# Key-feature exponentials queued behind the logits' exponentials, later LN2 norms, and PV in paced vacant slots, in a fused attention and GLU kernel

## The chip, the cores and the metric

The kernel runs on one core of one Trainium2 chip. The metric is the device time of one execution in microseconds (us). Every time quoted is a median of several executions. One profile is taken of each kernel. Its span is about 1.7 us shorter than the time of the same execution.

Engines are named as the profile names them: PE (TensorE, matmuls), PEld (its weight loads), DVE (VectorE), ACT (ScalarE), POOL (GpSimd) and SP (SyncE, which issues most transfers).

## The reference

One block, in bf16, on 2048 tokens of width 448 with 16 heads of 28 and a hidden width of 1792: a modulated layer norm, an attention that works in four segments of 512 tokens and carries a memory from one to the next, a second modulated layer norm (LN2), and a gated linear unit.

```python
h = layernorm(x) * (1 + ca) + sa
# attention, per segment s; M and z start at zero
logits = q_s @ k_s.T * scale + causal_mask
a_dot = softmax(logits) @ v_s
pq = phi(q_s)                            # phi(t) = t + 1 if t > 0 else exp(t)
a_mem = (pq @ M) / (pq @ z + 1e-6)
o_s = g * a_mem + (1 - g) * a_dot        # g = sigmoid(beta), per head
pk = phi(k_s)
M, z = M + pk.T @ v_s, z + sum(pk)
# after all segments
x = x + ga * (o @ wo)
h = layernorm(x) * (1 + cb) + sb
x = x + gb * ((sigmoid(h @ w_gate) * (h @ w_up)) @ w_down)
```

## The kernel before

The work is cut into units (segment s, group hc of four heads). Each unit's logits come in three groups g. Between these groups PE is fed with jobs from a queue, `fill`, by their estimated cost: projections of later segments, the gated unit of earlier ones. `later(ns, fn, tag)` puts off the emission of an instruction by so many ns of estimated PE time; `need(tag)` emits at once what is still put off. Delays of `later` are therefore not waits on the chip: they decide an instruction's place in its engine's order.

The features phi of keys and queries are an exponential on ACT, then a max-add (r) and a minimum (e) on DVE. Those of keys are then transposed by a DMA from SP into pk, from which the memory's update dM is computed. Both `phi` and the causal masks on POOL follow each unit's logits:

```python
def phi(src, wait, tag, then=None):
    e = work.tile([P, L], BF16, tag="e", bufs=5, name="e")
    nc.scalar.activation(e[:], src, AF.Exp)

    def fin():
        r = work.tile([P, L], BF16, tag="r", bufs=2, name="r")
        nc.vector.tensor_scalar(r[:], src, 0.0, 1.0, op0=ALU.max, op1=ALU.add)
        nc.vector.tensor_tensor(e[:], e[:], r[:], ALU.min)
        if then:
            then(e)
    later(wait, fin, tag)
    return e

def mem_k(s, hc):                        # one key feature
    ...
    phi(kT_of[s][:, hc, :], 3500 if s < 2 else 5000, ("pk", s),
        lambda e: nc.sync.dma_start_transpose(pk[:, hc, :, :], e[:]))

def mem_update(s):
    need(("pk", s))
    ...                                  # 16 matmuls: dM += pk.T @ v

def logits(s, hc, g):
    ...                                  # matmuls into lg
    nc.scalar.activation(pT[:, :, w0:w0 + wid], lg[:, :, 0:wid], AF.Exp, scale=scale)
    if g == 0 and s > 0:
        pq_of[u] = phi(qT[:, hc, :], 3600, ("pq", u))
    for kb in KB_GROUPS[g]:
        later(2600, lambda kb=kb: mask(pT, kb), ("mask", u))

def wo_fin(s, t):                        # LN2 of tile t
    ...
    ln.stats(t)
    ln.rstd(t, t + 1)                    # on POOL
    later(1500, lambda: ln.norm_t(t), ("ln2", s))   # on DVE, then a transpose from SP

def mem_jobs(s):
    return [(0, lambda: [later((2000 if s < 2 else 2500) * hc, lambda hc=hc: mem_k(s, hc), ("pk", s))
                         for hc in range(NHC)])] + [(16 * TR, lambda: mem_update(s))]

def prep_b1():                           # modulation for the second half
    ga = mod_rep(2, 1.0, "ga")
    wm[4] = load_wm((nc.sync,), 4)       # 392 KB each, from SP
    gb = mod_rep(5, 0.5, "gb")
    wm[3] = load_wm((nc.sync,), 3)
    ...
def prep_b2():                           # matmuls that read wm[3] and wm[4]
    mod_cols(((3, 2), (4, 3)))

# the queue of the early jobs; j0..j3 are projections of segments 0 to 3, m[s] = mem_jobs(s)
fill.extend(j1[8:] + [(1800, prep_b1)])
fill.extend(j2[:8] + m[0][1:])
fill.extend(j2[8:] + j3[:2] + [(2000, prep_b2)] + j3[2:])

# main loop, for each unit and each g
logits(s, hc, g)
...
if prev[0] >= 0 and (g == 1 or g == 0 and s > 1 and pace[0] + debt <= 0) and prev in todo:
    pv(*prev)                            # 40 matmuls: softmax(logits) @ v
```

The softmax here doesn't subtract the row's maximum and nothing guards it: scores larger than these inputs give would overflow.

## Time and profile before

| | kernel before |
|---|---|
| time, median of the first 3 runs | 259.19 us (258.83 to 259.82) |
| span of the profiled run | 257.9 us |
| PE busy | 242.2 us (94%) |
| DVE, ACT, POOL busy | 68%, 54%, 29% |
| mean granted clock of PE | 0.993 |

PE is the bound, so the views to read are PE's order in time with its idle times and what ended each, and the granted clock in the same stretches. In a row of the timeline, "[0.74 <-DMA pk<-e]" means that PE stood idle for 0.74 us just before it and that a transfer into pk ended this. The rows are shown in the prediction below.

### The profile page before, as it was taken

What the parts mean: (1) busy time and instruction counts of PE and PEld (TensorE: products, weight loads), DVE (VectorE), ACT (ScalarE), POOL (GpSimd) and SP (SyncE); (2) the same over time, 40 slices, a digit from 0 to 9 for tenths busy, and PEclk for the clock granted to TensorE, in tenths of its full rate; (3) what the DMA queues carried; (4) which work ended last, traced back from release to release, by engine and by line L of the source; (5) the groups of instructions that cost most, each with busy time, mean ns of one, the idle gap of its engine ahead of it and who ended that gap; (6) DMA issues with size and microseconds to landing.
All of it is one profiled execution on the core that took longest, in us unless ns stands there. A gap on an engine that the chain in (4) does not pass through costs nothing.

```text
span 257.9 us, 5314 instructions
## 1 busy us (share of the span) xinstructions
PE 242.2 (94%) x2056; PEld 114.9 (45%) x2083; DVE 175.5 (68%) x419; ACT 139.8 (54%) x173; POOL 75.2 (29%) x140
## 2 busy tenths in 40 slices
PE   7899996989996979999999999999999999999994
PEld 2434543446533344444544355454353455333453
DVE  6878899586786677988858756895664586544412
ACT  0368888759886696856359666543663200133300
POOL 4368045144345031352502140362020023000000
PEclk9999999999998999999999999999999999999999
DMA  5999996664032024111322400114210015100011
GB/s 145 290 257 269 340 246 120 84 160 84 3 62 45 20 42 64 20 23 20 58 69 53 81 19 4 23 25 96 56 22 3 0 20 119 36 0 0 3 36 36
DMA packets 41169, 19.66 MB, mean 76 GB/s; under 512 B 30009, under 2 KB 40249, under 8 KB 41145
## 3 DMA queue, kind: packets, MB, share of 16 engines
q1 hardware_dynamic: 38408, 17.61, 31.3%
q10 hardware_dynamic: 2736, 1.72, 2.3%
q8 instruction: 16, 0.26, 0.4%
q14 instruction: 9, 0.07, 0.1%
HBM read 10.67 MB, written 1.84 MB: 48 GB/s over the span
## 4 chain that ended last, share of the span: by engine, by line
PE 46%; DVE 10%; issue 2%; POOL 1%; DMA 1%; ACT 1%; SPq 0%; DVEq 0%; POOLq 0%
PE ups L551 12%; PE dps L566 11%; PE gps L534 10%; PE gps L539 4%; PE acc L443 3%; DVE fT L554 2%; PE lg L418 2%; DVE st L269 1%; PE pwo L502 1%; DVE x_sb L512 1%; DVE ot L568 1%; DMA hT<-xn 1%; PE ups L539 1%; PE dM L391 1%; POOL rs L274 1%
## 5 line engine op out<-in xcount | busy, mean ns | idle before, releaser
L421 ACT ACTIVATE pT<-lg 128x2048 bf16<-128x2048 f32 (+1 forms) x48 | 76.7, 1598 | 25.9 <-PE lg L418 21.4
L429 POOL TENSOR_SCALAR_AFFINE_SELECT pT<-pT 128x512 bf16<-128x512 bf16 x64 | 41.7, 667 | 71.1 <-ACT pT L421 71.1
L542 ACT ACTIVATE tt<-gps 128x512 f32<-128x512 f32 x56 | 30.5, 594 | 56.1 <-PE gps L539 56.1
L554 DVE SCALAR_TENSOR_TENSOR fT<-tt,ups 128x512 bf16<-128x512 f32 x56 | 37.1, 687 | 34.1 <-PE ups L551 32.7
L566 PE MATMUL dps<-wd_sb,fT 128*128 128x448 bf16 (+1 forms) x238 | 44.1, 342 | 0.5 <-DVE ot L568 0.5
L534 PE MATMUL gps<-hT,wg_sb 128*128 128x512 bf16 x155 | 41.0, 387 | 1.4 <-DVE hT L291 0.5
L551 PE MATMUL ups<-hT,wu_sb 128*128 128x512 bf16 x164 | 40.6, 381 | 0.4 <-issue 0.3
L566 PEld LDWEIGHTS <-fT 128*128 128x128 bf16 x238 | 22.8, 98 | 19.2 <-issue 0.6
L534 PEld LDWEIGHTS <-wg_sb 128*128 128x128 bf16 x168 | 15.9, 99 | 19.1 <-issue 1.5
L551 PEld LDWEIGHTS <-wu_sb 128*128 128x128 bf16 x168 | 14.1, 98 | 21.5 <-issue 7.7
L443 PE MATMUL acc<-vt,pT 128*128 128x29 bf16 x640 | 18.7, 175 | 3.2 <-POOL pT L429 2.1
L443 PEld LDWEIGHTS <-pT 128*128 128x128 bf16 x640 | 17.7, 96 | 6.4 <-POOL pT L429 2.7
L273 POOL TENSOR_SCALAR rs<-mv 128x1 f32<-128x1 f32 (+2 forms) x21 | 5.4, 257 | 50.8 <-DVE mv L270 50.8
L269 DVE BATCH_NORM_STATS2 st<-x_sb 128x6 f32<-128x448 bf16 x32 | 19.7, 616 | 0.5
L418 PE MATMUL lg<-qT,kT 28*128 28x512 bf16 (+3 forms) x256 | 17.3, 302 | 1.5 <-ACT pT L421 1.5
L539 PE MATMUL ups<-hT,wgu_sb 64*128 64x512 bf16 x56 | 17.8, 382 | 0.7 <-DVE fT L554 0.5
L568 DVE TENSOR_TENSOR ot<-dps,x_sb 128x448 bf16<-128x448 f32 (+1 forms) x17 | 10.1, 593 | 11.6 <-PE dps L566 11.6
L343 PE MATMUL pq<-hT,wq_sb 128*128 128x512 bf16 x58 | 16.3, 380 | 1.3 <-DVE ou L452 0.9
L539 PE MATMUL gps<-hT,wgu_sb 64*128 64x512 bf16 x56 | 17.1, 382 | 0.1
L277 DVE TENSOR_SCALAR xn<-x_sb,mv,rs 128x448 bf16<-128x448 bf16 x32 | 14.1, 460 | 3.6 <-POOL rs L274 3.6
L343 PE MATMUL pq<-hT,wk_sb 128*128 128x512 bf16 x61 | 16.3, 379 | 0.3
L370 DVE TENSOR_TENSOR e<-e,r 128x512 bf16<-128x512 bf16 x24 | 13.7, 573 | 2.4 <-ACT pT L421 0.5
(101 smaller groups left out, 259.8 us busy)
## 6 DMA issues: line engine op xcount, KB each, us to landing
wm<-in_w_mod_dram SPq DMA_DIRECT2D x4, 392.0 KB, 6.5
x_sb<-in_A_x_dram SPq DMA_DIRECT2D x3, 448.0 KB, 5.9
wd_sb<-in_B_w_down_dram SPq DMA_DIRECT2D x3, 448.0 KB, 9.5
wg_sb<-in_B_w_gate_dram SPq DMA_DIRECT2D x3, 448.0 KB, 9.7
wu_sb<-in_B_w_up_dram SPq DMA_DIRECT2D x3, 448.0 KB, 11.2
out_dram<-ot SPq DMA_DIRECT2D x8, 112.0 KB, 1.9
out_dram<-ot ACTq DMA_DIRECT2D x7, 112.0 KB, 1.7
wm<-in_w_mod_dram SPq DMA_DIRECT2D x2, 196.0 KB
```

The costliest lines, as they stand in the source:

```text
L269: nc.vector.bn_stats(st[:], self.srcs[i])
L343: nc.tensor.matmul(pq[:, 0:L], lhsT=head_cols(w_sb, k, hc), rhs=h[:, k, :], start=(k == 0), stop=(k == NK - 1))
L418: nc.tensor.matmul(lg[:, hs, wid:wid + nq], lhsT=kT[r, hc, kb * P:(kb + 1) * P], rhs=qT[r, hc, kb * P:L], start=True, stop=True, tile_posi ...
L421: nc.scalar.activation(pT[:, :, w0:w0 + wid], lg[:, :, 0:wid], AF.Exp, scale=scale)
L429: nc.gpsimd.affine_select(out=blk, in_=blk, compare_op=ALU.is_ge, fill=0.0, base=0, pattern=[[0, 4], [1, P]], channel_multiplier=-1)
L443: nc.tensor.matmul(accv[:, qb, hs, 0:ME], lhsT=pT[:, hs, c0:c0 + P], rhs=vt[:, kb, hc * 4 + hs, 0:ME], start=(kb == 0), stop=(kb == qb))
L534: nc.tensor.matmul(g[:, 0:L], lhsT=wg_sb[:, k, f], rhs=h[:, k, :], start=(k == 0), stop=False)
L539: nc.tensor.matmul(dst[:, 0:L], lhsT=wgu_sb[r:r + LW, f], rhs=h[r:r + LW, 3, :], start=first, stop=not first, tile_position=(r, 0))
L542: nc.scalar.activation(tt[:], g[:, 0:L], AF.Tanh, scale=0.5)
L551: nc.tensor.matmul(u[:, 0:L], lhsT=wu_sb[:, k, f], rhs=h[:, k, :], start=False, stop=(k == 2))
L554: nc.vector.scalar_tensor_tensor(ft[:], tt[:], 1.0, u[:, 0:L], op0=ALU.add, op1=ALU.mult)
L566: nc.tensor.matmul(dp[:, c], lhsT=fT_of[(s, fc)][:, t * P:(t + 1) * P], rhs=wd_sb[:, fc, c], start=(fc == 0), stop=(fc == NFC - 1))
```

## The change

The intent is threefold. Exponentials of key features no longer come at fixed intervals, but one behind each exponential of a unit's logits (g = 1 or 2, or 0 in segment 0), so that they don't gather in front of the next one. (The recorded texts call these exponentials short. Only that of g = 2 is: in segment 0 of the changed kernel those of g = 0, 1 and 2 take 1.88, 1.91 and 1.08 us.) LN2's norms are put off longer, so that they don't hold up DVE. And PV may take a vacant slot at g = 0 in segment 1 as well.

```diff
-        phi(kT_of[s][:, hc, :], 3500 if s < 2 else 5000, ("pk", s), lambda e: ...)
+        phi(kT_of[s][:, hc, :], 3500, ("pk", s), lambda e: ...)
+    kq = deque()
     def mem_update(s):
+        while kq:
+            kq.popleft()()
         need(("pk", s))
 ...
         if g == 0 and s > 0:
             pq_of[u] = phi(qT[:, hc, :], 3600, ("pq", u))
+        elif kq:
+            kq.popleft()()
 ...
-        later(1500, lambda: ln.norm_t(t), ("ln2", s))
+        later(1500 if s == NSEG - 1 else 2400, lambda: ln.norm_t(t), ("ln2", s))
 ...
     def mem_jobs(s):
-        return [(0, lambda: [later((2000 if s < 2 else 2500) * hc, lambda hc=hc: mem_k(s, hc), ("pk", s)) for hc in range(NHC)])] + [(16 * TR, lambda: mem_update(s))]
+        return [(0, lambda: kq.extend([lambda hc=hc: mem_k(s, hc) for hc in range(NHC)])),
+                (16 * TR, lambda: mem_update(s))]
 ...
-    fill.extend(j2[:8] + m[0][1:])
-    fill.extend(j2[8:] + j3[:2] + [(2000, prep_b2)] + j3[2:])
+    fill.extend(j2[:8])
+    fill.extend(j2[8:10] + m[0][1:] + j2[10:] + j3[:2] + [(2000, prep_b2)] + j3[2:])
 ...
-                if prev[0] >= 0 and (g == 1 or g == 0 and s > 1 and pace[0] + debt <= 0) and prev in todo:
+                if prev[0] >= 0 and (g == 1 or g == 0 and s > 0 and (hc > 1 or s > 1) and pace[0] + debt <= 0) and prev in todo:
 ...
-                    fill.extend(tail)
+                    fill.extend((m[s][0:1] if s < 3 else []) + tail)
 ... (the first job of m[1] and of m[2] is taken out of its old place)
```

More of the change, by code (lines that the diff above doesn't have):

```diff
@@ L379, in mem_k @@
         pk = pk_of[s]
-        phi(kT_of[s][:, hc, :], 3500 if s < 2 else 5000, ("pk", s), lambda e: nc.sync.dma_start_transpose(pk[:, hc, :, :], e[:]))
+        phi(kT_of[s][:, hc, :], 3500, ("pk", s), lambda e: nc.sync.dma_start_transpose(pk[:, hc, :, :], e[:]))
     rm_of = {}
+    kq = deque()
     def mem_update(s):
+        if kq:
+            print("forced kq", s, len(kq))
+        while kq:
+            kq.popleft()()
         need(("pk", s))
@@ L796 @@
                             gj = gj[:8] + m[2][1:] + gj[8:]
-                            dj = dj[:3] + m[2][0:1] + dj[3:]
                         fill.extend(dj[:3] + h2_jobs(s - 1) + dj[3:] + gj)
                     else:
-                        fill.extend(h2_jobs(s - 1) + m[1][0:1] + gj[:8] + m[1][1:] + gj[8:])
+                        fill.extend(h2_jobs(s - 1) + gj[:8] + m[1][1:] + gj[8:])
                     pace[0] = (cost(fill) - KEEP[s] * GU) / (12 if s < 3 else 9)
```

## The prediction

> **What bounds the kernel now.** I began with the page: its shares of busy time, then its slices for the clock.
>
> ```profile
> PE 242.2 (94%) x2056; PEld 114.9 (45%) x2083; DVE 175.5 (68%) x419; ACT 139.8 (54%) x173; POOL 75.2 (29%) x140
> PE 46%; DVE 10%; issue 2%; POOL 1%; DMA 1%; ACT 1%; SPq 0%; DVEq 0%; POOLq 0%
> ```
>
> TensorE (PE) is busy for 94% of 257.9 us, and in the chain that ended last it has by far the largest share. So the kernel is bound by the order and density of PE's work, and a change that touches no matmul can win only the time in which PE stands still. Next I read PE's timeline for those places. Rows with an idle time and a releaser, in order of time:
>
> ```profile
> 40.02 1.15 PE L443 MATMUL acc<-vt,pT 128*128 128x29 bf16 x40 [1.11 <-DVE kT L348]
> ...
> 44.56 1.04 PE L343 MATMUL pq<-hT,wq_sb 128*128 128x512 bf16 x3 [0.89 <-DVE ou L452]
> ...
> 55.21 0.38 PE L391 MATMUL dM<-vt,pk 128*128 128x116 bf16 x4 [0.74 <-DMA pk<-e]
> ...
> 79.53 1.15 PE L443 MATMUL acc<-vt,pT 128*128 128x29 bf16 x40 [1.76 <-POOL pT L429]
> ...
> 82.01 1.03 PE L534 MATMUL gps<-hT,wg_sb 128*128 128x512 bf16 x2 [0.51 <-DVE hT L291]
> ...
> 91.98 0.40 PE L418 MATMUL lg<-qT,kT 28*128 28x384 bf16 x8 [1.30 <-ACT pT L421]
> ...
> 98.83 0.37 PE L539 MATMUL ups<-hT,wgu_sb 64*128 64x512 bf16 x1 [0.28 <-DVE fT L554]
> 99.43 0.37 PE L539 MATMUL ups<-hT,wgu_sb 64*128 64x512 bf16 x1 [0.20 <-DVE fT L554]
> ```
>
> These eight waits are 6.8 us. The columns are start, duration, engine and line, operation, and in brackets PE's idle time and what ended it. All lie before 100 us; behind that no single wait of PE reaches 0.5 us (0.34 at 124, 0.48 at 253). Whatever the change does in segments 2 and 3 is therefore worth nearly nothing: the prize lies in segments 0 and 1. Last, the busy time by windows around the wait at 79:
>
> ```profile
> 80.00:82.00 2.00, 1.50 (x32) 0.82 (x28) 0.63 (x2) 0.98 (x3) 1.23 (x2) 0.82 0.45 91
> 82.00:84.00 2.00, 1.89 (x4) 0.72 (x6) 1.93 (x7) 0.60 (x2) 0.00 (x0) 0.50 0.05 12
> 84.00:86.00 2.00, 1.88 (x12) 0.53 (x12) 0.88 (x3) 0.89 (x2) 0.00 (x0) 0.83 0.00 0
> ```
>
> The columns are busy time (and count) of PE, weight load, DVE, ACT and POOL, then granted clock, DMA share and GB/s. The clock fell to half from about 81.3 to 84.7 us, just behind the idle stretch; that costs at most 3.4 x 0.5 = 1.7 us more.
>
> **What the Trainium skill says.** "TensorE: Matmul & The Clock Gate", Part 1: the clock is halved after an idle window of about 3.4 us, and the windows run freely. The trace agrees in the length (0.82, 0.50 and 0.83 over 6 us make 3.4 us at half); that a window with 1.76 us of waiting suffices is this trace's own finding. The same page, under "Architectural detail", calls ACT and DVE strict FIFO; the trace agrees, as an exponential of key features at 92.33 stands ahead of the one of the logits at 92.85, whose logits began at 91.98. "DMA: Bandwidth & Descriptors", section "Queues, rings and completion order": each DMA engine takes the descriptors of a ring in order. The trace fits: a transpose usually lands 2.4 us after its issue, but the one of oT issued at 55.16, behind the two 392 KB loads of wm (54.05 and 54.69), landed at 59.98, after 4.8 us.
>
> **The change part by part.** It adds no work: the order of the built programs has the same 4168 rows on PE, and on the others the same operations, moved. PE's order differs in two places only: dM of segment 0 comes after two tiles (8 matmuls) of the v projection instead of before them; and one PV (40 matmuls, of unit 2 of segment 1) comes before the second logits of unit 3 instead of after. The extended condition thus moves a single PV.
>
> 1. *Key features of segment 0, on DVE.* Each costs DVE one max-add and one min, by the rows of kT here 0.28 + 0.43 to 0.67 us. One pair (36.49 to 37.30, 0.8 us) stands before the kT copy of 39.31 that PE's PV waits for; in the new order it is behind it. The copy comes some 0.7 us earlier, limited by its own matmul: PE's wait of 1.11 shrinks to about 0.4, worth **0.7 us**. A second pair (41.80 to 42.85) stands between that PV and its ou (43.88); it moves behind it, so ou comes about 1 us sooner and the wait of 0.89 goes: **0.9 us**.
>
> 2. *dM of segment 0.* Its four pk tiles come by DMA transposes in the SP queue, one issue each 1.3 us (43.66, 45.05, 46.33, ...: the queue issues nearly back to back from 41 to 56 us). Now the exponentials stand one behind each short exponential, so the fourth is at about 45 us instead of 38.1, and its fin on DVE at about 49 instead of 45.1. In the new SP order the two wm loads and one oT come before the fourth pk, and the wm loads before the third. Before, the fourth pk was issued at 52.73 and landed at 55.17. If all else stays, it is issued after two loads (1.1 us) and one oT (1.3 us) more, less up to 1.5 us of gaps that close: about 53.6. It then lies behind 784 KB of loads; the oT of before took 4.8 us in that place, and those further back 4.0. So it lands at some 55.5 to 57.5, say 56.2. PE wants it: before at 54.4; two tiles later (+1.6), less the 1.6 of point 1, again at about 54.3. So a wait of roughly 1.9 to 2.3 takes the place of 0.74: **-1.3 us** as an estimate, and this is the least certain term.
>
> 3. *Later LN2 norms.* In segment 1 a norm with its copy (0.39 + 0.18 us) leaves the stretch of DVE before the last statistics (75.26). POOL's masks stand in its order behind the rs that waits for these statistics (idle 2.68 us at 76.19), and PE's PV at 79.53 waits for the masks. So PE gains about **0.55 us**. The last norm now follows the third in the time in which it waited for POOL (0.76 us), so hT isn't later; the wait at 82.01 stays. In segment 2 hT was ready at 132.05 and wanted at 134.14, which leaves room. In segment 3 it was ready at 180.33 and wanted at 180.68: 0.35 us of slack only, and I allow 0.1 of loss there.
>
> 4. *PV in the vacant slot, and the exponentials of segment 1.* At 90.69 PE had nothing but the second logits, which wait until ACT has emptied the first. ACT began that exponential at 90.05, behind one of key features (89.53), though its logits began at 88.68. Now the key feature isn't there: ACT can begin when its two tanh end (89.65), 0.4 us earlier. And the PV, 1.0 us of PE, whose masks were done at 87.8, fills the rest. 1.30 + 0.1 of pipeline refill: **1.4 us**.
>
> 5. *fT.* At 98 PE waits for buffers that DVE frees with fT at 98.10, behind two key-feature pairs (95 and 97). One pair moves behind the first fT pair and one leaves: the 0.48 us of the two waits go, with the gaps between starts perhaps 0.8. I take **0.6 us**.
>
> Sum: 0.7 + 0.9 - 1.3 + 0.55 - 0.1 + 1.4 + 0.6 = 2.75 us. As PE bounds everything after 100 us, this should pass to the end undiminished.
>
> **The rivals.** *(a) The new wait for pk is no worse than the old one*, because SP closes more gaps or the loads are done sooner. For it: 8 matmuls more were put ahead of dM for just this purpose. Against it: the order of SP and the late oT above. Then 1.3 to 2 us more are won: 254.4 to 255.2. *(b) The wait for pk is 3 us or more, and PE's clock falls there.* For it: 1.76 us sufficed at 79. It would cost up to 1.7 us: with 1 us of longer wait 258 to 259. *(c) The fall of the clock at 81 goes*, as the wait there shrinks from 1.8 to 1.2 us: up to 1.3 us won, since part of the half-speed window was idle anyway. The windows run freely, so this may differ from run to run, and the runs before spread by 1 us (258.83 to 259.82). *(d) ACT becomes the bound of 40 to 50 us*: it was busy for 14.6 of the 20 us from 40 to 60, and a fourth exponential now stands ahead of the q copy at 45.6. Some of point 1 would be lost, but as PE then waits for pk anyway, that costs nothing more.
>
> **Range and chances.** The median before is 259.19; less 2.75 is 256.4. (b) and (c) about balance, and (a) at one chance in four with 1.6 us pulls by 0.4; I allow half of that, as (d) pulls the other way: 256.2. All gains with (a) and (c) reach 253.3; only the PV with a bad wait and a slow clock gives 258.5. I put 8 in 10 at 253.9 to 258.4. Faster by over 2% needs under 254.0, so (a) together with most of (c): 0.11. Slower by over 2% (over 264.4) has no mechanism that I see: 0.02.
>
> **What would show it right or wrong.** Right: PE's waits at 40, 44.6, 92 and 98 gone or under 0.4 us; the PV of segment 1's third unit standing at 90 directly behind mem, followed by logits with no wait; the wait for masks near 77 at 1.2 to 1.3 us; a wait of dM for pk of about 2 us, with the third and fourth pk landing 3 us or more after their issue behind wm; no new PE wait over 0.4 us after 100 us. Wrong: if dM waits under 0.8 us, point 2 fails and the time is near 255; if it waits over 3, or a half-clock window stands at 55 us, the time is near 258. If hT of segment 3 arrives more than 0.5 us late, point 3 fails. And if these waits are gone but the span isn't shorter, PE wasn't the bound after 100 us.

## The result, and the profile after

The changed kernel is correct and took 262.75 us (median of 4 runs, 261.99 to 263.53) against 259.1 us for the kernel before. The ratio is 1.0136, with a 95% interval of 1.0095 to 1.0178. A ratio is the mean time of one kernel's runs over that of the other's runs of the same rounds, so not quite the ratio of the medians. The change made the kernel 1.4% slower. The prediction said 256.2 us, with 258.4 as the end of its range: it had the wrong sign.

The profile below is of the slowest of the four runs (263.53 us); the one of the kernel before is of a run of 259.59 us. The mean clocks of the four were 0.98, 0.992, 0.98 and 0.992. One window of 3.4 us at half clock takes 0.0065 off the mean of such a span; so, by this estimate, the profiled run's 0.98 means three such windows (two and one, below), and 0.992 about one, wherever it stood. The two runs of 0.992 took 261.99 and 262.25 us, still some 3 us more than the kernel before, whose profiled run had one window too. The term for the clock below is that of the profiled run, and larger than in these two.

From the page of the changed kernel, the busy times, the granted clock in 40 slices of 6.5 us, and the shares of the chain that ended last:

```profile
PE 245.6 (94%) x2056; PEld 115.9 (44%) x2083; DVE 175.7 (67%) x419; ACT 139.6 (53%) x173; POOL 75.6 (29%) x140
...
PEclk9999999985999799999999999999999999999999
...
PE 56%; DVE 8%; POOL 2%; issue 2%; ACT 1%; DMA 1%; DVEq 0%; POOLq 0%
```

PE has the same 2056 instructions but is busy for 3.4 us longer: some ran at half clock. The clock row shows where, at the slices of 52 to 65 us and of 85 to 91 us. PE is still the bound.

PE's timeline of the changed kernel, at the places shown before and at new ones (start, duration, engine, line, operation, and idle time before it with what ended it):

```profile
39.03 1.15 PE L451 MATMUL acc<-vt,pT 128*128 128x29 bf16 x40 [0.38 <-DVE kT L348]
...
42.92 1.02 PE L343 MATMUL pq<-hT,wq_sb 128*128 128x512 bf16 x3 [0.23 <-PE lg L424]
...
56.91 0.38 PE L397 MATMUL dM<-vt,pk 128*128 128x116 bf16 x4 [2.79 <-DMA pk<-e]
58.16 0.57 PE L397 MATMUL dM<-vt,pk 128*128 128x116 bf16 x4 [0.86 <-DMA pk<-e]
...
83.53 1.15 PE L451 MATMUL acc<-vt,pT 128*128 128x29 bf16 x40 [1.71 <-POOL pT L437]
...
94.34 1.16 PE L451 MATMUL acc<-vt,pT 128*128 128x29 bf16 x40
95.43 0.40 PE L424 MATMUL lg<-qT,kT 28*128 28x384 bf16 x8
...
143.41 0.39 PE L547 MATMUL ups<-hT,wgu_sb 64*128 64x512 bf16 x1 [0.49 <-DVE t L463]
...
186.73 0.39 PE L547 MATMUL ups<-hT,wgu_sb 64*128 64x512 bf16 x1 [0.52 <-DVE t L482]
```

The waits of 1.11, 0.89, 1.30, 0.28 and 0.20 are gone or small, as predicted. But dM's 0.74 became 2.79 + 0.86 = 3.65 us, the wait for masks did not shrink, and there are waits beyond 100 us that were not there before. The busy time by windows around dM (columns: busy time and count of PE, weight load, DVE, ACT, POOL, then granted clock, DMA share, GB/s):

```profile
54.00:56.00 2.00, 0.12 (x3) 0.00 (x0) 0.00 (x0) 0.26 (x1) 0.16 (x1) 1.00 1.32 271
56.00:58.00 2.00, 0.38 (x4) 0.22 (x4) 0.00 (x0) 0.00 (x0) 0.00 (x0) 0.88 0.98 188
58.00:60.00 2.00, 1.84 (x11) 0.79 (x12) 1.24 (x3) 0.61 (x1) 0.51 (x1) 0.50 0.08 16
60.00:62.00 2.00, 2.00 (x7) 0.81 (x6) 1.88 (x2) 2.00 (x3) 1.52 (x2) 0.50 0.01 4
```

All engines stand almost still from 54 to 58 us while the DMA engines are full; then PE works at clock 0.50 until about 64.35 us, which is two windows of 3.4 us.

The quickest way to place a loss is to compare the start of the same logits in both timelines. The difference, after minus before (taken before rounding), can only change where PE gained or lost:

| logits of (segment, unit, group) | before, us | after, us | lag, us | step, us | what lies between |
|---|---|---|---|---|---|
| 0, 0, 0 | 16.92 | 16.66 | -0.26 | | |
| 0, 3, 0 | 46.39 | 44.73 | -1.66 | -1.40 | DVE order in segment 0 |
| 1, 0, 0 | 57.04 | 58.66 | +1.62 | +3.28 | dM's wait for pk |
| 1, 1, 0 | 65.31 | 69.61 | +4.31 | +2.69 | half clock at 57.5 to 64.4 |
| 1, 2, 0 | 74.46 | 78.50 | +4.05 | -0.26 | LN2 norms |
| 2, 0, 0 | 99.73 | 101.26 | +1.53 | -2.52 | PV slot, fT; clock at 85 about equal |
| 3, 0, 0 | 144.20 | 147.19 | +2.99 | +1.46 | segment 2 |
| 3, 3, 1 | 186.33 | 190.29 | +3.95 | +0.96 | segment 3, at its end |

From there the lag stays to the end, as it does in all kernels below.

### The profile page after: what moved, and what is told of

It reads as the page before. It is cut to its first block, busy times and chain, and to the rows that moved or that the text cites. A ratio compares the mean times of both kernels' runs of the same rounds, so it can differ in the third digit from the quotient of the medians.

```text
span 261.8 us, 5314 instructions
## 1 busy us (share of the span) xinstructions
PE 245.6 (94%) x2056; PEld 115.9 (44%) x2083; DVE 175.7 (67%) x419; ACT 139.6 (53%) x173; POOL 75.6 (29%) x140
## 3 DMA queue, kind: packets, MB, share of 16 engines
q10 hardware_dynamic: 2736, 1.72, 2.3%
HBM read 10.67 MB, written 1.84 MB: 48 GB/s over the span
## 4 chain that ended last, share of the span: by engine, by line
PE 56%; DVE 8%; POOL 2%; issue 2%; ACT 1%; DMA 1%; DVEq 0%; POOLq 0%
PE ups L559 14%; PE dps L574 13%; PE gps L542 12%; PE gps L547 5%; PE acc L451 3%; PE pwo L510 3%; PE lg L424 3%; DVE fT L562 1%; POOL pT L437 1%; ACT pT L427 1%; DVE ot L576 1%; DMA hT<-xn 1%; DVE x_sb L520 1%; PE ups L547 1%; DVE st L269 1%
## 5 line engine op out<-in xcount | busy, mean ns | idle before, releaser
L343 PE MATMUL pq<-hT,wq_sb 128*128 128x512 bf16 x58 | 17.0, 393 | 0.8 <-issue 0.4
L355 PE MATMUL pv<-wv_sb,hT 128*128 128x448 bf16 x64 | 15.4, 389 | 0.0
```

The costliest lines, as they stand in the source:

```text
L343: nc.tensor.matmul(pq[:, 0:L], lhsT=head_cols(w_sb, k, hc), rhs=h[:, k, :], start=(k == 0), stop=(k == NK - 1))
```

## The experiments

All kernels gave correct results. Most edits below are to the changed kernel.

**Were the wm loads to blame for dM's wait?** First the issues of transfers between 47 and 60 us (size in KB, median us from issue to landing), of the kernel before:

```profile
wm<-in_w_mod_dram SPq DMA_DIRECT2D x2, 392.0 KB, 4.1
...
pk<-e SPq DMA_TRANSPOSE x2, 2.4
```

and of the changed kernel, followed by SP's own timeline there:

```profile
wm<-in_w_mod_dram SPq DMA_DIRECT2D x2, 392.0 KB, 4.3
pk<-e SPq DMA_TRANSPOSE x3, 4.6
```

```profile
51.14 1.07 SPq L120 DMA_DIRECT2D wm<-in_w_mod_dram  x2
52.30 1.20 SPq L380 DMA_TRANSPOSE pk<-e  x1
53.55 1.27 SPq L498 DMA_TRANSPOSE oT<-ou  x1
54.91 1.22 SPq L380 DMA_TRANSPOSE pk<-e  x1
```

The third and fourth pk now stand behind both loads. The profile has landings for one pk in each of these stretches: 2.4 us for that of 52.73 before, 4.6 us for the third now. The fourth let PE go on at 58.16, 3.25 us after its issue. In e1 both loads are issued after the last pk, in e1b only one of them, and e2 leaves the wait but fills it with 16 matmuls whose result is thrown away, so that the clock can't fall.

```diff
 # e1                                       # e1b: the wm[3] line alone
-        wm[4] = load_wm((nc.sync,), 4)
-        wm[3] = load_wm((nc.sync,), 3)
 ...in mem_update
         need(("pk", s))
+        if s == 0:
+            for j in (4, 3):
+                wm[j] = load_wm((nc.sync,), j)
 # e2, in mem_update, ahead of the third pk
+            if s == 0 and hc == 2:
+                idle = m_f32("idle")
+                for _ in range(16):
+                    nc.tensor.matmul(idle[:, 0:L], lhsT=ident[:], rhs=hT_of[("1", 2)][:, 0, :], start=True, stop=True)
```

> The changed kernel, with its two 392 KB loads of wm issued on SP behind the fourth pk of segment 0 instead of ahead of the third; the exponentials stay where the change put them. Theory A (the transposes of pk queue behind the loads): the third and fourth pk land about 2.5 us after their issue, dM waits for pk under 1 us instead of 2.79 + 0.86, no half-clock windows stand at 57 to 64 us, and 262.75 falls by about 2.7 + 2.6 to 257 or 258. Theory B (the exponentials queued behind each short one come too late, the loads are innocent): dM still waits over 2 us, the clock still falls, and the time stays at 262 or more.

> The changed kernel with one of the two wm loads (the second) moved behind the pk transposes, the other left ahead of them: the dose between the changed kernel (both ahead, waits for pk 2.79 and 0.86 us) and e1 (none ahead, wait 2.02, no half-clock window). Theory (each load that stands ahead delays the transposes by its own share): wait about 2.8 us in sum, one half-clock window, 260 to 261 us, ratio 1.004 to 1.008. Rival (only the order in the queue counts, not the bytes: one issue of 0.6 us): wait 2.6 to 2.7 at most and no window, ratio 1.002 or less. Other rival (one load is as bad as two): as the changed kernel, 1.012.

> The changed kernel with 16 dummy matmuls of 512 columns (3.45 us, their result is not used) between the second and third head group of dM in segment 0, where PE waits for pk. Nothing waits less, so without a clock effect the time is that of the changed kernel, 262.7, or a little more. Theory A' (the empty stretch of PE makes the clock fall for the next two windows): the clock stays at full speed from 54 to 65 us and the time falls by about 2.6 us to 260.1. Rival (the clock falls for another reason): still two half-speed windows near 57 to 64 us, and 262.7 or more.

| kernel | time, us | ratio to before (95%) | dM's wait, us (profiled run) | half-clock windows behind it (profiled run) |
|---|---|---|---|---|
| changed | 262.75 | 1.0136 (1.0095 to 1.0178) | 3.65 | 2 |
| e1b, one load ahead | 261.64 | 1.009 (1.005 to 1.0129) | 1.84 + 0.78 = 2.62 | 2 |
| e1, none ahead | 258.69 | 0.999 (0.9951 to 1.0029) | 2.02 | 0 |
| e2, wait filled | 261.91 | 1.0112 (1.0077 to 1.0148) | 0.64 beside the fill | 0 |

dM in e1's timeline, and the windows there:

```profile
56.09 0.38 PE L400 MATMUL dM<-vt,pk 128*128 128x116 bf16 x4 [2.02 <-DMA pk<-e]
```

```profile
54.00:56.00 2.00, 0.07 (x2) 0.00 (x0) 0.00 (x0) 0.01 (x1) 0.00 (x0) 1.00 0.40 81
56.00:58.00 2.00, 1.91 (x15) 1.02 (x16) 1.49 (x3) 1.08 (x1) 0.76 (x1) 1.00 0.86 216
```

The loads cost 1.6 of the 3.65 us, and with them, in the profiled runs, come the two windows at half clock. The remaining 2.0 us is SP's queue: in e1 the last pk is still issued only at 53.6 us, because the pk, hT and oT transposes leave SP one per 1.3 us. Neither of the two theories given for e1 was right in all: A in the landings (2.4 us) and the clock, not in its wait of under 1 us; B in a wait of over 2 us, not in the clock. e1b shows that the clock falls with a wait split in two parts of 1.84 and 0.78 us as well; it was slower than its theory said (260 to 261). e2 shows the clock's part in its profiled run: with the same long stretch at dM, but filled, no window at half clock follows, and at the third logits of segment 1's first unit its lag is 1.44 us where the changed kernel has 4.31. At the start of segment 3's second unit it is -0.2 against +2.99; 0.3 us of this comes of the window at 85 us, which e2's run lacks too. Its time missed the theory (261.91 instead of 260.1): 1.4 us was lost again in segment 3, where its step is +2.34 us instead of +0.96 (a late transpose; last section), and four of its six runs had mean clocks of 0.985 to 0.992, so that they had windows somewhere.

How many windows follow is not fixed by the wait. e3 and e12 (below) have the program of the changed kernel up to this place. In their profiled runs dM waited 2.98 + 0.82 and 3.28 + 0.73 us, longer than in the changed kernel, and one window at half clock followed instead of two: 1.63 and 1.69 us of lag, where the two cost 2.69.

**Is segment 0 the whole difference?** e10 puts segment 0 alone back: key features of s = 0 at the old intervals, dM at its old place.

```diff
+        if s == 0:
+            return [(0, lambda: [later(2000 * hc, lambda hc=hc: mem_k(s, hc), ("pk", s)) for hc in range(NHC)]), (16 * TR, lambda: mem_update(s))]
-    fill.extend(j2[:8])
-    fill.extend(j2[8:10] + m[0][1:] + j2[10:] + j3[:2] + ...)
+    fill.extend(j2[:8] + m[0][1:])
+    fill.extend(j2[8:] + j3[:2] + ...)
```

> The changed kernel with segment 0 alone put back: its key features at the old fixed intervals, dM at its old place, the rest of the change kept. Theory (the loss is the sum of its places: segment 0 with dM's wait and the two half-clock windows +4.2, norms -0.3, PV slot and fT -2.3, segment 2 +1.5, segment 3 +1.0): minus 4.2 against the changed kernel, so 258.5 to 259.2, ratio about 1.000, with dM's wait about 0.7 us and no half-clock window at 57 us. Rival (segment 0's waits only push a later loss about, so that what is won there is given back): 261 or more.

It took 257.38 us, ratio 0.994 (0.9899 to 0.9981), with a wait of 0.19 us at dM and a mean clock of 1.0. So segment 0 turns the change from a gain into a loss. It did 1.1 us better than the theory's 258.5. In its trace the step in segment 2 was 0.3 us instead of 1.5, though the order there is that of the changed kernel; dM's wait was 0.19 us where 0.7 was expected; and there is no half-clock window near 81 us, as there is in the kernel before.

**What was lost in segment 2?** e4 puts the key features of segment 2 back to the old intervals.

> The changed kernel with the key features of segment 2 alone put back to the times of before (every 2500, fin after 5000, begun after three down jobs). Theory D (the waits of PE at 138.0 and 143.4 us, 0.36 and 0.49, come of the key-feature pairs of segment 2 standing ahead of the copies that free PSUM on DVE): those waits go and the time falls by 1.2 to 1.5 us, to about 261.3. Rival (they come of the later norms): unchanged, 262.7.

It took 261.9 us, ratio 1.0091 (1.0053 to 1.0129); theory D had said 261.3. In its trace the lag stays constant through segment 2 (0.36 to 0.30 us): the 1.5 us are due to the new order of segment 2. But e10 has that order and lost little. The same stretch in DVE's timeline of the changed kernel, then in POOL's:

```profile
140.80 0.76 DVE L369 TENSOR_SCALAR r<-qT 128x512 bf16<-128x512 bf16 x1
141.59 0.73 DVE L370 TENSOR_TENSOR e<-e,r 128x512 bf16<-128x512 bf16 x1
```

```profile
140.78 1.27 POOL L437 TENSOR_SCALAR_AFFINE_SELECT pT<-pT 128x512 bf16<-128x512 bf16 x2 [2.62 <-ACT pT L427]
```

and of e10, again DVE, then POOL:

```profile
134.90 0.28 DVE L369 TENSOR_SCALAR r<-qT 128x512 bf16<-128x512 bf16 x1
135.22 0.42 DVE L370 TENSOR_TENSOR e<-e,r 128x512 bf16<-128x512 bf16 x1
```

```profile
135.24 1.49 POOL L437 TENSOR_SCALAR_AFFINE_SELECT pT<-pT 128x512 bf16<-128x512 bf16 x2 [2.62 <-ACT pT L427]
```

In the changed kernel the pair of query features starts 20 ns after two masks on POOL and takes 1.49 instead of 0.70 us. In e10 it starts first, and the masks take 1.49 instead of 1.27. Only the masks have moved: the pair starts 0.88 and 0.87 us after PE's PV in the two traces, the masks 0.86 and 1.21 us after it. The Trainium skill states this in "SBUF — State Buffer", section "Who interferes with whom": a DVE instruction in a two-port mode contends with GpSimd, one with two inputs in SBUF with a GpSimd instruction that reads SBUF, and whichever issues first holds the other up. The trace agrees in both directions. Behind the slowed pair stand the three instructions that free the accumulator of PV, for which PE then waited 0.49 us. This was tested by moving that pair alone; on no other engine does the order change.

```diff
 # e12
-            pq_of[u] = phi(qT[:, hc, :], 3600, ("pq", u))
+            pq_of[u] = phi(qT[:, hc, :], 4600 if u == (2, 3) else 3600, ("pq", u))
```

> The changed kernel with one pair of DVE instructions (max-add and min of the query features of segment 2's fourth unit) moved behind the three that free the accumulator for PE; nothing else moves on any engine. Theory (segment 2's larger wait, 0.49 us at 143.4, comes from DVE and GpSimd meeting: the pair took 0.76 + 0.73 us beside two masks at 140.78 to 142.05, against 0.28 + 0.42 in the same order where they do not meet): the wait of 0.49 goes, the step of 0.77 us in the lag between the second and the third logits of that unit goes, and 0.7 to 0.8 us of it reaches the start of segment 3; the wait of 0.36 us at 138 stays. In the time -0.3%: ratio about 1.010. Rival (the accumulator's release is late for another reason, such as the late release of the two buffers before it): the step stays at 0.5 us or more.

In e12's DVE timeline the pair is back at its usual length:

```profile
140.94 0.28 DVE L369 TENSOR_SCALAR r<-qT 128x512 bf16<-128x512 bf16 x1
141.25 0.42 DVE L370 TENSOR_TENSOR e<-e,r 128x512 bf16<-128x512 bf16 x1
```

The wait of 0.49 us is gone, and the step between the second and the third logits of the unit is -0.10 instead of +0.77 us. The other, 0.7 us before the second logits, stayed, as expected. The time was 261.94 us, ratio 1.01 (1.0064 to 1.0136). e12 by itself doesn't tell the collision from the order, as it also takes the pair's ordinary 0.70 us out of the way. e10 does: there the pair stands in the changed kernel's place at its usual length, PE has no wait of 0.49 us, and the lag stays at -3.68 between the second and the third logits. The two together show that half of segment 2's loss (0.77 us) is the collision. The other half comes with the new order too (e4 removes it); 0.36 us of it is a wait behind DVE, in which a pause of 0.46 us between r and e stands that no run explains. e10 hasn't this pause, and its step there is 0.39 instead of 0.75 us.

**LN2's norms.** e11 is the kernel before with the later norms alone, e3 the changed kernel with the norms of segment 2 (whose LN2 runs during segment 3) at the old 1500.

```diff
 # e11, on the kernel before
-        later(1500, lambda: ln.norm_t(t), ("ln2", s))
+        later(1500 if s == NSEG - 1 else 2400, lambda: ln.norm_t(t), ("ln2", s))
 # e3, on the changed kernel
-        later(1500 if s == NSEG - 1 else 2400, lambda: ln.norm_t(t), ("ln2", s))
+        later(2400 if s < 2 else 1500, lambda: ln.norm_t(t), ("ln2", s))
```

> The kernel before with the later LN2 norms alone (2400 instead of 1500, the last segment left). The prediction's step: the wait for masks near 79 us shrinks by 0.55 us and that passes to the end, 258.4, ratio 0.998. Theory after seeing the two traces: only about 0.3 us, 258.7, ratio 0.999, which five rounds hardly tell from nothing; so the trace decides: the wait at 79.5 us 1.76 in the kernel before, 1.2 by the prediction, 1.5 by the later theory.

> The changed kernel with the LN2 norms of segment 3 (those of s = 2) deferred by 1500 again, as before the change; segments 1 and 2 keep 2400. Theory C (three hT transposes now queue behind each other at 175.7 to 178.3 us, and what comes of it is PE's wait of 0.37 at 184.9 and 0.52 at 186.7): both waits shrink under 0.3 us and the time falls by 0.7 to 1.0 us, to about 261.9. Rival (these waits come of DVE's order around the key features of segment 2 or of chance): no change, 262.7.

e11 took 259.55 us, ratio 1.0021 (0.9985 to 1.0058). Its PE rows:

```profile
79.01 1.18 PE L443 MATMUL acc<-vt,pT 128*128 128x29 bf16 x40 [1.70 <-POOL pT L429]
...
180.89 0.81 PE L534 MATMUL gps<-hT,wg_sb 128*128 128x512 bf16 x3 [0.37 <-DVE ot L568]
...
182.75 0.39 PE L539 MATMUL ups<-hT,wgu_sb 64*128 64x512 bf16 x1 [0.52 <-DVE t L474]
```

The wait for masks is as long as before (1.76), and the two waits of the changed kernel's segment 3 are there. So this part alone wins 0.26 us of order in segment 1 and loses 1 us in segment 3. The masks' wait stays because no norm left the place ahead of the last statistics: In the kernel before, DVE has a norm at 74.09 and these statistics at 75.26; in e11 it has one at 73.34 and the statistics at 74.51. Each norm only moved down by one place, and the one before it took its place. Why it loses is seen on SP and DVE. The changed kernel, SP, then DVE:

```profile
174.41 0.33 SPq L577 DMA_DIRECT2D out_dram<-ot  x1
175.74 3.81 SPq L287 DMA_TRANSPOSE hT<-xn  x3
```

```profile
180.90 0.74 DVE L291 TENSOR_SCALAR hT<-hT,cols 128x512 bf16<-128x512 bf16 x2 [3.72 <-DMA hT<-xn]
```

The later norms put the last three transposes behind an output and back to back, 1.3 us each. The last lands at 180.8 us, and DVE, whose next instruction needs it, waits 3.72 us (3.00 before) with everything behind it. e3 took 262.06 us, ratio 1.0124 (1.0079 to 1.0168): in its trace the waits and the step of 0.96 us are gone, as theory C said, but the time moved by less than the spread that the clock makes (its runs had mean clocks of 0.974 to 0.987).

**PV's slot.** e5 is the kernel before with the new condition for PV alone.

```diff
-  (g == 1 or g == 0 and s > 1 and pace[0] + debt <= 0)
+  (g == 1 or g == 0 and s > 0 and (hc > 1 or s > 1) and pace[0] + debt <= 0)
```

> The kernel before with one part of the change alone: the PV of segment 1's third unit in the slot ahead of the second logits of its fourth. Theory E (the slot was empty: PE waited 1.30 us there for ACT): that wait shrinks to about 0.5, as the exponential of key features still delays ACT, PE is about 1.0 us ahead at the third logits of that unit, and the time falls by 0.8 to 1.0 us to about 258.1. Rival (what is won is lost at once in the two waits for fT at 98 us, since DVE isn't faster): these waits grow from 0.48 to over 1 us and the time falls by less than 0.4 us.

It took 257.44 us, ratio 0.9952 (0.992 to 0.9984). Its lag against the kernel before goes from -0.50 us at the start of the third unit of segment 1 to -2.34 at the start of segment 2, and stays; 0.36 us of this comes before the slot, 1.49 in it and behind it. PE's wait of 1.30 us became 0.30 there and 0.47 at the next logits, and the two waits for fT are gone, though the key features are the old ones. This line is the one part of the change that is shown to win by itself.

**The good parts together.** e6 is the changed kernel with e1, e3 and e4 together. e7 and e8 take dM further back, behind all of segment 2's v tiles, to end the 2 us of waiting; e8 also asks for the masks of segment 1 earlier. e9 is e7 with the modulation matmuls `prep_b2` four jobs later.

```diff
 # e7
-    fill.extend(j2[8:10] + m[0][1:] + j2[10:] + j3[:2] + [(2000, prep_b2)] + j3[2:])
+    fill.extend(j2[8:] + m[0][1:] + j3[:2] + [(2000, prep_b2)] + j3[2:])
 # e8, besides
-            later(2600, lambda kb=kb: mask(pT, kb), ("mask", u))
+            later(1300 if s == 1 else 2600, lambda kb=kb: mask(pT, kb), ("mask", u))
 # e9, in place of e7's line
+    fill.extend(j2[8:] + m[0][1:] + j3[:6] + [(2000, prep_b2)] + j3[6:])
```

> The changed kernel with three repairs at once: wm loads behind the fourth pk, the norms of segment 3 and the key features of segment 2 as before the change. If the three causes are separate and add up (theory of the account): 258.7 of the run with the wm loads behind pk, less about 1.0 for segment 3 and 1.5 for segment 2: 256.2, a ratio of 0.989 to the kernel before. Rival (they overlap, because PE waits elsewhere once one is gone): 257.5 or more.

> The three repairs, and dM of segment 0 two more v tiles (8 matmuls, 1.5 us) later. In the run with the wm loads behind pk, dM still waited 2.02 us for the fourth pk, which SP issued at 53.59 behind five transposes in a row. Theory (PE is simply too early for a queue that issues one transpose per 1.3 us): the wait falls from 2.0 to about 0.5 us and the time by 1.5 us against the three repairs alone, to about 254.7. Rival (rm then comes too late for the first memory read, or a clock window decides): less than 0.7 us.

> As the one with dM later, and the masks of segment 1 put on POOL 1300 instead of 2600 after their logits, so that two of the three masks which the PV near 79 us waits for stand ahead of the last rs instead of behind it. Theory (that PV waits for POOL's order, not for POOL's speed): its wait falls from 1.72 to about 0.5 us, the half-clock window behind it goes in most runs, and the time falls by 1.2 to 2 us against the same kernel without this, to about 253. Rival (POOL now waits for ACT ahead of rs, and the norms come later): no gain, or PE waits more for hT than 0.4 us.

> As e7 (the mix with dM of segment 0 behind all of segment 2's v tiles), but the modulation matmuls that waited 3.52 us for the wm loads now come four projection jobs (4 us of PE) later. Theory (the wait in e7 is only a matter of the loads' landing at 63.3 us against PE's arrival at 59.9): dM's wait about 0.2 us, no wait for wm, no half-clock window at 63, so that the 2.0 us of dM's wait that the mix e6 still had are now won as well: about 254.4 us, ratio 0.982 to 0.985. Rival (PE's time lost there is lost to something that follows the waits around, such as masks or hT, so that shortening one lengthens the next): 256 or more, not better than e6, with a wait elsewhere in segments 0 or 1 longer by some 1.5 us.

| kernel | time, us | ratio to before (95%) |
|---|---|---|
| e6 | 256.21 | 0.991 (0.9877 to 0.9943) |
| e7 | 259.63 | 1.0015 (0.9985 to 1.0045) |
| e8 | 259.8 | 1.0032 (1.0004 to 1.0059) |
| e9 | 253.27 | 0.977 (0.9735 to 0.9805) |

e6 met its number, 256.2: the parts add up. e7 and e8 were misses. The modulation row of e7's PE timeline, then dM and the wait for hT in e9's:

```profile
63.37 0.48 PE L228 MATMUL cp<-silu,wm 112*128 112x1 bf16 x12 [3.52 <-DMA wm<-in_w_mod_dram]
```

```profile
57.26 0.38 PE L400 MATMUL dM<-vt,pk 128*128 128x116 bf16 x4 [1.19 <-DMA pk<-e]
...
80.74 1.89 PE L545 MATMUL gps<-hT,wg_sb 128*128 128x512 bf16 x4 [1.29 <-DVE hT L291]
```

In e7 the wait for pk fell to 0.23 us, but the wm loads, now issued at 56.5 us, were still under way when `prep_b2` needed them: a wait of 3.52 us, and two half-clock windows behind it. In e8 the masks came earlier indeed, but PE's wait of 1.72 us at the same place was then ended by DVE's t, not by POOL; nothing was won. e9 gives the loads their time: no wait for wm, and 1.19 us at dM (0.2 was expected). Its wait for masks is down to 0.40 us, but behind it PE now waits 1.29 us for hT, as the rival of its expectation said of such waits. It had a mean clock of 0.999 or 1.0 in five of its six runs; the profiled one is the sixth (255.45 us, 0.993, one half-clock window). It is the fastest kernel, below both the kernel before and the changed one. Whether it is faster by 2% stays unclear, as its interval reaches 0.9805.

## Why the prediction was wrong

The sum of the prediction's terms was -2.75 us; the trace's steps add up to +4.21. Term by term:

| term of the prediction | predicted, us | in the trace, us | |
|---|---|---|---|
| 1. DVE's order in segment 0 | -1.6 | -1.40 | right |
| 2. dM waits for pk | +1.3 | +3.28 | mis-sized |
| (b) clock falls there | 0 in the sum | +2.69 | took place |
| 3. norms, segment 1 | -0.55 | -0.26 | half, by another way |
| 3. norms, segment 3 | +0.1 | +0.96 | mis-sized |
| 4 and 5. PV slot and fT | -2.0 | -2.52 | right in sum |
| segment 2 | 0 | +1.46 | not seen |

- **Point 2 failed first, in its size.** The mechanism, pk behind the wm loads in SP's order, was right, and the prediction called it its least certain term. It put the last pk at 56.2 us. The fourth pk was issued at 54.91, not 53.6, because the gaps of SP's queue that were to close by up to 1.5 us didn't: transposes keep leaving one per 1.3 us. It then took 3.25 us to let PE go on, where 2.6 had been reckoned. So PE's wait for it ended at 58.16 instead of 56.2, and the whole was 3.65 us (2.79 for the third pk, 0.86 for the fourth) instead of 1.9 to 2.3. PE arrived nearly as predicted (54.1 us, against 54.3). e1 and e1b give the loads' share, 1.6 of the 3.65 us. Some 0.3 us of the +3.28 is already the half clock, which began at 57.5.
- **Rival (b) came true, and had no weight in the sum.** The prediction gave the fall of the clock at most 1.7 us and balanced it against rival (c). That is the size of one window: it cost 1.63 us in e3 and 1.69 in e12. In the profiled run of the changed kernel there were two, and 2.69 us; that one or two follow the same program differs from run to run, and the mean clocks above say that it did so here. With (b) the prediction named 258 to 259 us; even that was too little by about four. Rivals (a) and (c) did not take place in the profiled run: dM's wait was longer, and the wait at 83.5 us was as long as before and a half-clock window follows it still. Rival (d) wasn't seen: the waits of point 1 fell as reckoned.
- **"Segments 2 and 3 are worth nearly nothing" was the other wrong step.** It was drawn from the waits of the kernel before: no wait there means that nothing can be won. It does not mean that nothing can be lost. The change moved DVE and SP instructions there too. The prediction itself had found only 0.35 us of slack in segment 3 and allowed 0.1 us for it; the loss was 0.96 us. In segment 2, 0.77 us came from DVE and POOL meeting, which e12 removed; 0.7 us more came with the new order.
- **Point 3's gain** assumed that a norm leaves the way to the last statistics on which POOL's masks hang. In e11 another norm takes its place there, and the masks' wait stayed at 1.70, against 1.2 to 1.3 predicted. The 0.26 us came elsewhere, ahead of the third unit's first logits.
- **Points 1 and 4 were right** in mechanism and nearly in size: the waits at 40, 44.6 and 92 are gone or under 0.4 us, and PV stands where it was said to. Point 5's waits at 98 are gone as well, but they are gone in e5 too, with the key features left where they were; so PV's move suffices for it, and what the moved key features add isn't shown.
- **What the prediction said would show it wrong did:** a wait over 3 us, a half-clock window at the place, new PE waits beyond 100 us, and hT of segment 3 some 0.7 us late (DVE could go on with it at 180.90 instead of 177.19, while PE's lag was 2.99).

What stays open: the 0.46 us pause between r and e, the 1.0 us of e9's dM wait above its expectation, and what decides between one window and two behind dM.

## What to carry to other kernels

When a change delays the producer of a transfer, write down the whole queue that issues it, with every transfer that now stands ahead and the time that each issue takes (1.3 us per transpose here), before trusting a gap to close; a wait that leaves PE idle for 3 to 4 us, as here, can cost 1.6 to 2.7 us more by the clock, so fill it or move the consumer. An absence of waits in a stage shows that nothing can be won there, not that nothing can be lost: look for the slack of every instruction that the change moves on side engines. Before dropping a change that lost, undo it part by part: here one line alone won 0.5%, and the kept parts with the consumers moved to where their data is ready won 2.3% (1.95 to 2.65).

## What the Trainium skill lacked or had wrong

- "TensorE: Matmul & The Clock Gate", section "Why this matters for your kernels", advises no idle gaps over about 3 us between bursts of matmuls. Here gaps of 1.84 and 0.78 us (e1b) and 2.79 and 0.86 us (the changed kernel) were followed by two half-clock windows, gaps of 3.28 and 0.73 us (e12) by one, and one of 1.76 us in the kernel before by one; but a single one of 2.02 us (e1) was followed by none. The section has no figure for a window that is only partly idle, which is the case here.
- "DMA: Bandwidth & Descriptors" has no time for the issue of one transpose from SBUF to SBUF on trn2; beside figures for a later chip it gives the sequencer cycles of earlier generations, for a single large transpose. In these traces one takes 1.2 us of SP and the next follows 1.3 us after it, whatever waits for it; in e1 this alone made PE wait 2.02 us.
- No page was found that says how much a fetch of instructions can delay a DMA transpose. In e2, the stretch of 175 to 179.5 us holds one such packet, and two hT transposes took 4.0 us, so that DVE waited 5.33 us for hT (3.72 in the changed kernel); the changed kernel has no such packet in the same stretch, and three took 2.4. That the one delays the other is read from these rows and was not tested by itself. The rows of e2's transfers in its stretch (queue, packets, MB, share; then median us from issue to landing), then the changed kernel's:

```profile
q8 instruction: 1, 0.02, 1.7%
...
hT<-xn SPq DMA_TRANSPOSE x2, 4.0
```

```profile
hT<-xn SPq DMA_TRANSPOSE x3, 2.4
```
